# Digit searches with fixed thresholds for the capacity routing of an attention and mixture-of-experts kernel

## Chip, cores and metric

One NeuronCore of a Trainium2 chip. The metric is the device time of one execution in microseconds (us), the median of the runs shown.

## What is computed

Attention over 8 batches, 8 heads, 576 positions and head width 64, with a threshold on the scores, then a mixture of experts over the 4608 rows that come out. Each expert takes exactly 576 rows, in the order of the logits:

```python
scores = scale * q @ k^T
scores = where(scores >= max(scores) - tau, scores, -1e9)
x      = softmax(scores) @ v                     # 4608 rows of 512
logits = x @ w_gate                              # 4608 x 8
for (token, e) in descending order of logits:    # greedy assignment
    if token is free and expert e holds < 576 tokens: assign
for e in range(8):
    out[rows of e] = relu(x[rows of e] @ w1[e]) @ w2[e]
```

## The kernel before

**Stages.** The attention runs until about 446 us: 64 pairs of heads are worked in slots of two score tiles, with TensorE, VectorE and ScalarE in a pipeline written out by hand. GpSimd adds tau to each tile's maximum (`mx`, line 76, tile `nb`), which the masking on VectorE (`stt`, line 91) needs one slot later. Then eight FFN rounds follow, one per expert, each with 12 x 16 matmuls of layer 1 (line 884) and a layer 2 (line 916); every operand is split into a high and a low part, so the corrections (`H`, `w1l`, `w2l`, `xl`, made by `tensor_tensor` through line 429) run on VectorE beside the matmuls.

**Searches.** The greedy assignment is done in rounds: each token's key `b` is its best logit among the open experts; the largest threshold is searched at which some expert has 576 tokens with a key at or above it; that expert closes with those tokens, and the next round follows. The tokens lie as 128 partitions x 36 columns. A search (`phase`, line 648) has seven levels. One level: `step_cmp` compares all keys with 32 or 16 thresholds (VectorE, `cmp`); `step_cnt` counts per threshold and expert with nine matmuls (line 500) and copies the counts (`cn`, `cm` or `cs`, by how late the search is); `step_flag` sums them with small matmuls (lines 517 and 519) and sets a flag per threshold (`jka`); `step_n` counts the flags with another matmul (lines 535, 549) and derives the next thresholds. Levels 0 to 2 work with tables (`E`, 34 thresholds in fp32), levels 3 to 6 with `scalar_tensor_tensor` of 1152 fp32 elements, whose added offset stands in PSUM (search 0) or in a small tile `sd`. `pick` and `rank1` then give the expert `e`, `pack` gives the row list `idx` with one-hot compares (`poh`, line 610).

**Search 0** (`alone`) follows the attention directly. Its first 31 columns are prepared and compared in the attention's `tail` (line 321), the last five after the last logits. Beside it run 30 deferred row units (`xt_unit`, line 243): four transposes on TensorE, two evictions on ScalarE and a store of up to 260 KB to `xrows`, through two PSUM banks and eight buffers. A loop (lines 380 to 384) interleaves them by time in the program's own costs: a search step when its time has come, else a row unit each `XTY` us. The gather of expert 0's rows (line 798, GpSimd) needs `idx` and the stored rows; its first weights are loaded from the ScalarE queue (line 737).

**Searches 1 to 6** run beside the FFN matmuls. `place` (line 934) starts them one after the other; a search waits until the FFN three rounds before is done, and pauses while the rows of round 1 are taken. Each step yields a delay from costs written out in `Vec`, and the FFN matmuls issued until then stand in front of the step's matmuls in TensorE's queue. Corrections wait in `fills`: one is issued in each gap of a search, or when a matmul wants it.

```python
            twice=n=="tensor_tensor" and out.dtype==BF16 and ins[0].dtype==BF16      # L423
            t=max(s.free,s.now)
            if any(x.name==s.last for x in ins): t=max(t,s.done)
            s.free=t+0.07+big/(1.9 if twice else 0.96)/1000+(0.0 if acc is None else 0.09)
            s.done=s.free+0.115                                                      # L428
    def wait(s): return max(0.0,s.done-s.now)+s.lat                                  # L417
LATS=[0.15,0.35,0.35]+[0.6]*5                                                        # L701
```

Of the kernel before, what the change touches and what calls it, by code (L numbers as in the profile page):

```python
# [19 lines left out]
PPB=8; LTB=1; VTB=4; HOLD=1; XW=520; NBO=2; NDEF=4; XTB=4; XTY=1.05; XT0=-1.2; XRB=2  # L20


def attention(ctx, tc, qk, vl, wgd, xrows, xts, Lg, nb_batches, ident, dup, idle, R, after_first):
# [364 lines left out]
NC_=36; J=32; CAP=576; BIGS=8192.0; RC=1.5*2.0**28; NH=20; ADDS=3  # L388

def const_arrays():  # L390

    k=np.zeros((128,4096),np.float32); o={}; pos=0
    def put(name,a):
        nonlocal pos
        a=np.asarray(a,np.float32)
# [2 lines left out]
    e=[2.0**(-126+16*i) for i in range(16)]
    put("E1",np.array([-FMAX]+[-x for x in reversed(e)]+e+[FMAX]))
    put("pw",np.array([2.0**i for i in range(J+2)])); put("nw",np.array([2.0**-i for i in range(J+2)]))  # L400
    put("lev",2.0**(1-5.0*np.arange(1,6)))
    lw=np.tile(2.0**(1-5.0*np.arange(1,6)),(128,1)); lw[0,4]=0; put("lew",lw)
    put("io",np.arange(J+2)); put("io4",np.arange(J+2)/16)
# [29 lines left out]
class Router:  # L433
# [8 lines left out]
    def setup(s,ident):  # L442
# [9 lines left out]
        x=ident.rearrange("p (c t) -> p c t",c=4); V.tensor_reduce(s.own,x,axis=AX.X,op=ALU.add)  # L452
        with s.nc.allow_low_precision(reason="one term of each sum is not zero"): V.tensor_reduce(s.sum,x.rearrange("p c t -> p t c"),axis=AX.X,op=ALU.add)
    def consts(s):
        V=s.V; G=s.G
# [23 lines left out]
    def compare(s,E0,js,c0=0,c1=NC_):  # L479
        n=c1-c0  # L480
        s.V.tensor_tensor(s.cmp.rearrange("p (c j) -> p c j",j=J)[:,c0:c1,:js],s.b[:,c0:c1].unsqueeze(2).to_broadcast([128,n,js]),E0[:,1:js+1].unsqueeze(1).to_broadcast([128,n,js]),op=ALU.is_ge)
    def step_cmp(s,E):
        V=s.V; lv=E["lv"]; s.js=js=16 if lv in (0,1) else J
        if lv>1:


            o=1 if lv<5 else 0
            V.scalar_tensor_tensor(s.cmp.rearrange("p (c j) -> p c j",j=J),s.st[:,lv-2,o:o+J].unsqueeze(1).to_broadcast([128,NC_,J]),E["add"],s.b.unsqueeze(2).to_broadcast([128,NC_,J]),op0=ALU.add,op1=ALU.is_le)
            return
        s.compare(E["E"],js,31 if s.alone and lv<0 else 0)  # L490
        if lv==1:

            s.hb=s.wk.tile([128,5],BF16,name="hb"); V.tensor_scalar(s.hb,s.k("lew"),s.ab,None,op0=ALU.mult)
            s.st=s.wk.tile([128,4,J+2],F32,name="st"); s.lo=E["lo"]
            V.scalar_tensor_tensor(s.st,s.k("io").unsqueeze(1).to_broadcast([128,4,J+2]),s.ab,s.k("lev")[:,1:5].unsqueeze(2).to_broadcast([128,4,J+2]),op0=ALU.mult,op1=ALU.mult)
# [28 lines left out]
    def step_n(s,B):

        V=s.V
        lv=B["lv"]
        ps=s.ps()
        if lv>0:


            d=ps[:,0:1]
            for l in range(lv,0 if s.alone else lv-1,-1):
                k=32 if l==5 else 128
                s.T.matmul(d,s.hb[0:k,l-1:l].to_broadcast([k,128]),s.jk[:,8:9] if l==5 else s.fl[:,l+1:l+2],start=(l==lv),stop=(l==1 or not s.alone))
            if not s.alone and lv<5:
                sd=s.wk.tile([128,1],F32,name="sd",bufs=3)
                if lv==1: V.tensor_copy(sd,d)
                else: V.tensor_tensor(sd,B["add"],d,op=ALU.add)
                d=sd  # L540
            if lv<5: return {"add":d,"lv":lv+1}
            s.T.matmul(ps[:,1:10],s.ones[0:32],s.jk,start=True,stop=True)
            lo=s.wk.tile([128,1],F32,name="lo5",bufs=2)
            if s.alone: V.tensor_tensor(lo,s.lo,d,op=ALU.add)
            else: V.scalar_tensor_tensor(lo,d,B["add"],s.lo,op0=ALU.add,op1=ALU.add)
            return {"lo":lo,"lv":6,"full":ps}
        E2=s.wk.tile([128,J+2],F32,name="E",bufs=3)
        n=ps[:,0:1]
        s.T.matmul(n,s.ones,s.fl[:,lv+1:lv+2],start=True,stop=True)
        sm=s.wk.tile([128,2],F32,name="sm",bufs=3); lo=sm[:,0:1]  # L550
        jk=s.wk.tile([128,J+2],F32,name="jk2")
        V.scalar_tensor_tensor(jk,s.k("io"),n,B["E"],op0=ALU.is_equal,op1=ALU.mult,accum_out=lo)
        if lv==-1:

            V.tensor_scalar(E2,s.k("pw"),lo,FMAX,op0=ALU.mult,op1=ALU.min)
            V.scalar_tensor_tensor(E2,s.k("nw"),lo,E2,op0=ALU.mult,op1=ALU.max)
        else:
            s.ab=sm[:,1:2]
            V.scalar_tensor_tensor(s.ab,lo,-1.0,lo,op0=ALU.mult,op1=ALU.max)
            V.tensor_scalar(E2,s.k("io4"),s.ab,lo,op0=ALU.mult,op1=ALU.add)  # L560
        return {"E":E2,"lo":lo,"lv":lv+1}
# [499 lines left out]
```

## Time and profile before

| | us |
|---|---|
| median of three runs | 967.71 (966.82 to 968.75) |
| profiled execution, its own time | 965.63 |
| its span, first to last instruction | 963.9 |
| granted TensorE clock, mean | 0.996 |
| busy: TensorE, VectorE, ScalarE, GpSimd | 936.5, 775.7, 638.3, 277.7 |

A row of the profile gives engine, line, operation, tiles and shapes, and the time in us. In a timeline the first column is the start, the second the duration (a row with a count spans from the first start to the last end), and in brackets the idle time before and what ended it. PE is TensorE, DVE is VectorE, ACT is ScalarE, POOL is GpSimd, SP is the sync engine. VectorE operations of the searches and corrections all carry line 429, so they are told apart by their tiles.

### The profile page before, as it was taken

To read this page: it belongs to the slowest core of one execution; us is meant where nothing else is said; L and a number is where in the kernel's file an instruction comes from. 1 tells how busy PE (TensorE), PEld (TensorE's weight loads), DVE (VectorE), ACT (ScalarE), POOL (GpSimd) and SP (SyncE) were. 2 spreads that over 40 slices of the span, in tenths; PEclk is the share of its full clock that TensorE was granted. 3 is DMA by queue.
4 is the path that set the end of the run, shared out by engine and by line. 5 is a ranking of instruction groups with operands and counts; after the bars stand their busy time and mean duration, and the time that the engine had idled before them with its cause. 6 is when DMAs were issued, how large, how long until landed. Compare 5 with 4: busy or idle time off the path is not lost.

```text
span 963.9 us, 24282 instructions
## 1 busy us (share of the span) xinstructions
PE 936.5 (97%) x9182; PEld 700.8 (73%) x9182; DVE 775.7 (80%) x2177; ACT 638.3 (66%) x1301; POOL 277.7 (29%) x485
## 2 busy tenths in 40 slices
PE   7999999999999999998889999999999999999996
PEld 4565666566566656565778797897988979898994
DVE  8999999999999999996778787788897978536220
ACT  6999999999999999996645343443543525455430
POOL 3434354353534343340020302113041323310101
PEclk9999999999999999999999999999999999999999
DMA  6322252533432333205752505325342516530101
GB/s 260 124 101 88 85 195 93 205 127 111 168 111 101 125 102 123 88 2 193 251 181 74 191 18 173 107 90 175 105 154 94 168 49 215 183 103 32 39 12 44
DMA packets 36293, 117.02 MB, mean 121 GB/s; under 512 B 4304, under 2 KB 4944, under 8 KB 35664
## 3 DMA queue, kind: packets, MB, share of 16 engines
q1 hardware_dynamic: 28784, 93.89, 27.9%
q0 software_dynamic: 5888, 19.03, 6.3%
q10 hardware_dynamic: 1504, 2.54, 0.9%
q8 instruction: 73, 1.20, 0.5%
q14 instruction: 44, 0.36, 0.1%
HBM read 93.01 MB, written 21.38 MB: 119 GB/s over the span
## 4 chain that ended last, share of the span: by engine, by line
PE 84%; DVE 7%; issue 5%; DMA 2%; POOL 0%; ACT 0%; POOLq 0%; ACTq 0%; DVEq 0%
PE pf L884 19%; PE pf L916 18%; PE sc L70 15%; PE xo L156 14%; PE tb L99 9%; PE sc L99 2%; PE xo L166 2%; PE pt L825 1%; DVE cmp L429 1%; DVE z L75 1%; DVE pp L91 1%; PE rps L500 1%; DMA out_dram<-y,idx 1%; PE xo L178 1%; DMA xg<-xrows,idx 1%
## 5 line engine op out<-in xcount | busy, mean ns | idle before, releaser
L75 DVE TENSOR_SCALAR_CACHE_REDUCE z<-sc 128x576 f32<-128x576 f32 x288 | 205.9, 752 | 15.1 <-PE sc L70 13.1
L76 POOL TENSOR_SCALAR nb<-nb,wg 128x1 f32<-128x1 f32 x288 | 144.8, 504 | 248.1 <-DVE z L75 185.5
L87 ACT ACTIVATE pp<-z,nb 128x576 f32<-128x576 f32 x256 | 192.9, 773 | 24.0 <-DVE z L75 20.7
L91 DVE SCALAR_TENSOR_TENSOR pp<-z,nb,pp 128x576 f32<-128x576 f32 x256 | 200.0, 814 | 0.0
L916 PE MATMUL pf<-w2h,H 128*128 128x512 f32 x576 | 191.5, 398 | 1.9 <-DVE H L429 1.9
L70 PE MATMUL sc<-qk 64*128 64x288 f32 (+1 forms) x1280 | 177.8, 421 | 1.0 <-DVE z L75 0.8
L156 PE MATMUL xo<-pt,vt 128*64 128x320 f32 (+1 forms) x1024 | 155.7, 420 | 0.0
L117 ACT ACTIVATE pt<-tb 128x512 f32<-128x512 f32 x253 | 137.7, 591 | 1.9 <-PE tb L99 1.3
L916 PE MATMUL pf<-w2l,H 128*128 128x512 f32 x320 | 128.4, 401 | 0.4 <-DVE w2l L429 0.4
L924 POOL DMA_INDIRECT out_dram<-y,idx x40 | 44.2, 1105 | 289.4 <-ACT y L919 188.0
L916 PEld LDWEIGHTS pf<-w2h,H 128*128 128x128 f32 x576 | 107.4, 189 | 22.4 <-DVE H L429 2.3
L70 PEld LDWEIGHTS sc<-qk 64*128 64x128 f32 (+1 forms) x1280 | 93.1, 177 | 27.9 <-DVE z L75 3.9
L884 PE MATMUL pf<-xl,w1h 128*128 128x288 f32 (+2 forms) x512 | 110.1, 299 | 0.0
L884 PE MATMUL pf<-xh,w1h 128*128 128x288 f32 (+2 forms) x512 | 109.9, 299 | 0.1
L884 PE MATMUL pf<-xh,w1l 128*128 128x288 f32 (+2 forms) x512 | 110.0, 299 | 0.0
L99 PEld LDWEIGHTS tb<-ident,pp 64*128 64x128 f32 x2032 | 75.2, 140 | 44.9 <-issue 18.9
L156 PEld LDWEIGHTS xo<-pt,vt 128*64 128x64 f32 x1024 | 60.7, 136 | 58.4 <-issue 32.4
L919 ACT ACTIVATE y<-pf 128x512 f32<-128x512 f32 x40 | 23.9, 598 | 117.2 <-PE pf L916 111.7
L896 ACT ACTIVATE hf<-pf 128x576 f32<-128x576 f32 x56 | 36.5, 653 | 89.4 <-PE pf L884 83.5
L99 PE MATMUL tb<-ident,pp 64*128 64x64 f32 x2032 | 91.9, 227 | 3.3 <-ACT pt L117 3.0
L798 POOL DMA_INDIRECT xg<-xrows,idx x40 | 51.1, 1278 | 132.3 <-PE pf L884 45.7
L884 PEld LDWEIGHTS pf<-xh,w1h 128*128 128x128 f32 x512 | 81.8, 188 | 1.0 <-ACT xh L826 0.3
(206 smaller groups left out, 1358.2 us busy)
## 6 DMA issues: line engine op xcount, KB each, us to landing
qk<-qk_dram SPq DMA_DIRECT2D x31, 864.0 KB, 4.5
vt<-vl_dram SPq DMA_DIRECT2D x32, 576.0 KB, 3.7
w2s<-w_dram SPq DMA_DIRECT2D x32, 512.0 KB, 5.5
w1s<-w_dram SPq DMA_DIRECT2D x28, 512.0 KB, 5.8
xrows<-pp SPq DMA_DIRECT2D x24, 260.0 KB, 2.3
xts<-xt SPq DMA_DIRECT2D x2, 1152.0 KB, 5.6
pt<-xts SPq DMA_DIRECT2D x2, 1152.0 KB, 6.9
xrows<-xr SPq DMA_DIRECT2D x8, 260.0 KB, 2.2
```

The lines of the kernel that those rows point to most:

```text
L70: T.matmul(sc[o,f,:HS], kd["q",h][r,c], kd["k",h][r,:],start=True,stop=True)
L75: V.tensor_scalar(z,SC.pop(t)[:,:,:HS],-0.125,None,op0=ALU.mult,op1=ALU.min,accum_out=nb[:,0:1])
L76: G.tensor_scalar(nb[:,1:2],nb[:,0:1],taub[:,0:1],None,op0=ALU.add)
L87: A.activation(pview(t),ZB[t].rearrange("p a b -> p (a b)"),AF.Exp,bias=NBI[t][:,0:1],scale=-1.0)
L91: V.scalar_tensor_tensor(pv,ZB.pop(t).rearrange("p a b -> p (a b)"),NBI[t][:,1:2],pv,op0=ALU.is_le,op1=ALU.mult,accum_out=den_of(p)[:,p%4/ ...
L99: g=slice(64*r,64*r+64); T.transpose(o[:,r],x[r%len(x)][g],ident[g,g])
L117: else: A.activation(o,tb,AF.Copy)
L156: T.matmul(xo[64*h:64*h+64,:q.stop-q.start],v[:,f,128*u+64*h:128*u+64*h+64],PT[p][:,h,u,q],start=new,stop=last,skip_group_check=True)
L798: G.indirect_dma_start(out=x[:n],out_offset=None,in_=xrows,in_offset=IOA(ap=s["idx"][:n,t:t+1],axis=0))
L884: T.matmul(ps[:,h,:n],s[w][:,k,f*128:(f+1)*128],s[x][:,k,cols[h]],start=(i==0),stop=(i==11))
L916: T.matmul(ps[:,0,:],H[:,f,c:c+128],s[w][:,f],start=(f==0 and j==0),stop=e)
L924: G.indirect_dma_start(out=out,out_offset=IOA(ap=s["idx"][:n,t:t+1],axis=0),in_=y[:n],in_offset=None)
```

## The change

Each key's bits are turned into an unsigned order and cut into seven digits of 5, 5, 5, 5, 4, 4 and 4 bits (`digits`: three operations on 36 columns and three on 7 x 36). A level compares a bf16 number `e` per key with thresholds that never change (`th`): `e` starts as the first digit, and each level takes off the threshold that was found and adds the next digit, scaled by 1/64 per level. So a key above the found prefix stays above all thresholds, and one below it stays below. Level 0 of search 0 compares the fp32 keys with 32 fp32 thresholds (`E0`, by `compare`, with one instruction for whole groups of four columns and one for each cut group). Four levels have 32 thresholds, three have 16. In the first three searches `cmp` is laid out with four columns innermost, in the later ones as before with the thresholds innermost. The tables, `hb`, `st` and `sd` are gone. The thresholds and scales are built once, mostly on GpSimd (`consts`). The row units stand 0.9 instead of 1.05 us apart in the program's costs.

```diff
-PPB=8; LTB=1; VTB=4; HOLD=1; XW=520; NBO=2; NDEF=4; XTB=4; XTY=1.05; XT0=-1.2; XRB=2
+PPB=8; LTB=1; VTB=4; HOLD=1; XW=520; NBO=2; NDEF=4; XTB=4; XTY=0.9; XT0=-1.2; XRB=2
...
-        R.prep(0,31); R.compare(R.k("E1"),J,0,31)
+        R.prep(0,31); R.compare(0,31)
         both_ev(b,x[:,:,384:],slice(0,64),V); V.tensor_copy(rd[64:128,:,4],RD[b-1][64:128,:,4])
+        for g in R.digits(0,31): g()
...
+SHL=(0,5,10,15,20,24,28); SHR=(27,)*4+(28,)*3; JS=(32,)*4+(16,)*3; NL=7
...
     def consts(s):
...
+        s.th=[t("th%d"%l,[128,n,4],BF16) for l,n in enumerate(JS)]; s.unit=t("unit",[128,NL],BF16); s.sh=t("sh",[128,2,NL],I32)
+        G.iota(s.th[0],pattern=[[1,32],[0,4]],base=1,channel_multiplier=0,allow_small_or_imprecise_dtypes=True)
+        for l in range(NL):
+            G.memset(s.unit[:,l:l+1],64.0**-l)
+            for i,n in enumerate((SHL[l],SHR[l])): G.memset(s.sh[:,i,l:l+1],n)
+            if l: G.tensor_scalar(s.th[l],s.th[0][:,:JS[l]],64.0**-l,-64.0**-l if l==NL-1 else 0.0,op0=ALU.mult,op1=ALU.add)
...
+    def digits(s,c0=0,c1=NC_):
...
+        return [lambda: V.tensor_scalar(z,s.b[:,c0:c1],0.0,None,op0=ALU.add),
+            lambda: V.tensor_scalar(k,zi,31,-2**31,op0=ALU.arith_shift_right,op1=ALU.bitwise_or),
+            lambda: V.tensor_tensor(k,zi,k,op=ALU.bitwise_xor),
+            lambda: V.tensor_tensor(d,k.unsqueeze(1).to_broadcast([128,NL,n]),w(s.sh[:,0]),op=ALU.logical_shift_left),
+            lambda: V.tensor_tensor(d,d,w(s.sh[:,1]),op=ALU.logical_shift_right),
+            lambda: V.tensor_tensor(D,d,w(s.unit),op=ALU.mult)]
+    def compare(s,c0=0,c1=NC_):
...
+    def step_cmp(s,l):
+        V=s.V; s.js=m=JS[l]
+        if s.alone and l==0: s.compare(31); return
+        e=s.e if l else s.D[:,0]
+        if s.count>ADDS: V.tensor_tensor(s.cmp.rearrange("p (c j) -> p c j",j=J)[:,:,:m],e.unsqueeze(2).to_broadcast([128,NC_,m]),s.th[l][:,:,0].unsqueeze(1).to_broadcast([128,NC_,m]),op=ALU.is_ge)
+        else: V.tensor_tensor(s.cmp.rearrange("p (g j c) -> p g j c",j=J,c=4)[:,:,:m],e.rearrange("p (g c) -> p g c",c=4).unsqueeze(2).to_broadcast([128,9,m,4]),s.th[l].unsqueeze(1).to_broadcast([128,9,m,4]),op=ALU.is_ge)
...
+    def step_n(s,l):
+        V=s.V; ps=s.ps(); n=ps[:,0:1]; m=s.js; u=s.unit[0:m,l:l+1].to_broadcast([m,128])
+        if l<NL-1:
+            s.T.matmul(n,u,s.fl[0:m,l:l+1],start=True,stop=True)
+            e=s.wk.tile([128,NC_],BF16,name="e0",bufs=3)
+            V.scalar_tensor_tensor(e,s.e if l else s.D[:,0],n,s.D[:,l+1],op0=ALU.subtract,op1=ALU.add)
+            s.e=e; return
+        s.T.matmul(n,u,s.jk[0:m,8:9],start=True,stop=True)
+        s.T.matmul(ps[:,1:10],s.ones[0:m],s.jk[0:m],start=True,stop=True)
...
     def phase(s,last=False):
...
+            todo=s.digits(31 if s.alone else 0)
+            def work(n):
+                while n and todo: todo.pop(0)(); n-=1
+            if not s.alone: work(6)
...
+            for l in range(NL):
+                s.step_cmp(l); work(3); yield gap()
+                held(0.34); s.step_cnt(); work(2); yield gap()
                 if s.count<=ADDS: held(0.16)
+                s.step_flag(l); work(1); yield gap()
+                held(0.1); E=s.step_n(l)
                 if not s.alone: yield V.ease()
```

`pick` and `rank1` compare the last `e` instead of `b`. In `setup`, `own`, `sum` and `eye` are built in the new order of columns; `tri` takes the identity from SBUF instead of from the loaded constants, of which the tables are gone.

## Rows read from the trace of the kernel before

**Rows 1.** Busy time by stage, whole kernel. Columns: the stretch and its length, then busy us of PE, PEld (weight loads), DVE, ACT and POOL with their instructions, the granted clock, the share of the 16 DMA engines and GB/s.

```profile
8.00:60.00 52.00, 48.29 (x598) 28.76 (x598) 51.90 (x147) 47.24 (x89) 20.94 (x45) 1.00 0.42 152
60.00:440.00 380.00, 379.87 (x4828) 230.57 (x4825) 363.82 (x1014) 359.85 (x726) 156.70 (x344) 1.00 0.33 113
448.00:480.00 32.00, 26.86 (x347) 22.05 (x348) 22.07 (x77) 20.05 (x61) 0.00 (x0) 1.00 0.76 259
480.00:500.00 20.00, 16.19 (x175) 14.61 (x173) 14.16 (x42) 9.91 (x27) 6.58 (x6) 1.00 0.63 200
500.00:587.00 87.00, 86.61 (x669) 76.56 (x668) 73.43 (x201) 41.21 (x87) 11.23 (x11) 1.00 0.32 105
587.00:596.00 9.00, 7.14 (x47) 5.02 (x46) 5.15 (x18) 1.64 (x3) 4.24 (x4) 0.81 0.30 94
596.00:920.00 324.00, 323.83 (x2250) 285.90 (x2249) 231.00 (x637) 144.23 (x284) 71.78 (x62) 1.00 0.35 117
```

**Rows 2.** The chain of waits between 464 and 490 us, in order of time. Columns: start, length, engine, tile and line. L500 is the count, L247 a row unit's transposes, L519 and L535 the small matmuls, L250 and L251 a row unit's evictions.

```profile
464.64 1.44 DVE cmp L429
...
466.12 0.39 PE sc L500 x9
466.51 0.48 PE xo L247 x4
...
467.09 0.52 PE xo L247 x4
467.61 0.09 PE sc L535 x4
...
472.46 0.48 ACT pp L250
472.94 0.10 ACT pp L251
...
474.53 5.84 DMA w1s<-w_dram
...
480.62 2.29 POOL xg L798
...
488.82 1.23 PE pf L884 x6
```

**Rows 3.** Timeline of VectorE from 441 to 486 us: preparation of the keys, search 0, packing, and the first scaling of gathered rows.

```profile
441.74 0.42 DVE L429 TENSOR_TENSOR q<-Lg,b 128x248 bf16<-128x248 f32 x1
...
447.40 0.36 DVE L209 TENSOR_TENSOR lw<-sc,rd 128x64 f32<-128x64 f32 x2 [2.66 <-PE sc L99]
...
452.09 0.26 DVE L429 SCALAR_TENSOR_TENSOR jk<-cst,sc 128x34 f32<-128x34 f32 x1 [0.36 <-PE sc L549]
...
452.68 0.25 DVE L429 SCALAR_TENSOR_TENSOR E<-cst,sm,E 128x34 f32<-128x34 f32 x1
452.96 0.76 DVE L429 TENSOR_TENSOR cmp<-b,E 128x576 bf16<-128x576 f32 x1
...
471.13 0.15 DVE L429 TENSOR_TENSOR lo<-sm,sc 128x1 f32<-128x1 f32 x1 [0.75 <-PE sc L542]
...
471.93 0.15 DVE L429 TENSOR_SCALAR e<-m 128x1 int32<-128x1 f32 x1
...
474.17 0.76 DVE L429 TENSOR_TENSOR poh<-pio,prb 128x1152 bf16<-128x1152 bf16 x1
...
478.22 0.17 DVE L429 SCALAR_TENSOR_TENSOR idx<-cps,ih 128x5 int32<-128x5 f32 x1
...
485.29 0.69 DVE L429 TENSOR_TENSOR xg<-xg 128x512 f32<-128x512 f32 x1 [1.62 <-DMA xg<-xrows,idx]
```

**Rows 4.** What the sync engine's queue waited for between 430 and 500 us. Columns: total, times, longest. Line 773 stands behind the last row store.

```profile
SPq L773 <- DMA xrows<-pp: 5.4, 1, 5.4
```

**Rows 5.** Timeline of VectorE from 620 to 645 us: a compare of search 3 and the copy of its counts (`cs`), and two operations of the preparation of search 4.

```profile
621.02 1.42 DVE L429 SCALAR_TENSOR_TENSOR cmp<-st,sd,b 128x1152 bf16<-128x1152 f32 x1
623.55 0.15 DVE L429 COPY cs<-rps 32x8 f32<-32x8 f32 x1 [1.11 <-PE rps L500]
...
642.18 0.31 DVE L429 TENSOR_TENSOR q<-q,w8b 128x288 bf16<-128x288 bf16 x1
...
643.01 0.46 DVE L429 TENSOR_TENSOR oh<-q,qm 128x288 bf16<-128x288 bf16 x1
```

**Rows 6.** Timeline of all engines from 587 to 590 us: search 3's first compare and the layer 2 matmul that waits.

```profile
587.38 1.35 DVE L429 TENSOR_TENSOR cmp<-b,cst 128x1152 bf16<-128x1152 f32 x1
...
589.39 0.50 PE L916 MATMUL pf<-w2h,H 128*128 128x512 f32 x1 [1.86 <-DVE H L429]
```

**Rows 7.** Timeline of all engines from 34 to 40 us: GpSimd's constants, the delayed `nb`, and the masking on VectorE that needs it.

```profile
34.38 0.68 POOL L458 TENSOR_SCALAR w8b<-cst 128x8 bf16<-128x8 f32 x1
...
35.41 0.09 POOL L461 MEMSET fla<- 128x6 bf16 x1
35.47 0.39 POOL L463 IOTA pio<- 128x128 bf16 x1
...
35.94 0.30 POOL L464 TENSOR_SCALAR pio<-pio 128x128 bf16<-128x128 bf16 x1
...
37.01 1.17 POOL L76 TENSOR_SCALAR nb<-nb,wg 128x1 f32<-128x1 f32 x2
...
39.32 0.81 DVE L91 SCALAR_TENSOR_TENSOR pp<-z,nb,pp 128x576 f32<-128x576 f32 x1
```

More of the change, by code (lines that the diff above doesn't have):

```diff
@@ L397, in put @@
         k[:a.shape[0],pos:pos+a.shape[1]]=a; o[name]=(pos,a.shape[1]); pos+=a.shape[1]
[L398 to L403, printed above, removed]
+    top=[(n<<27)^(1<<31) if n>=16 else ~(n<<27)&0xffffffff for n in range(1,32)]
+    put("E0",np.append(np.array(top,np.uint32).view(np.float32),np.finfo(np.float32).max))
     put("w8",8-np.arange(8))
@@ L451, in setup @@
         s.own=t("own",[128,4],F32); s.sum=t("sum",[128,32],F32R)
-        x=ident.rearrange("p (c t) -> p c t",c=4); V.tensor_reduce(s.own,x,axis=AX.X,op=ALU.add)
-        with s.nc.allow_low_precision(reason="one term of each sum is not zero"): V.tensor_reduce(s.sum,x.rearrange("p c t -> p t c"),axis=AX.X,op=ALU.add)
+        V.tensor_reduce(s.own,x.rearrange("p j c -> p c j"),axis=AX.X,op=ALU.add)
+        with s.nc.allow_low_precision(reason="one term of each sum is not zero"): V.tensor_reduce(s.sum,x,axis=AX.X,op=ALU.add)
     def consts(s):
@@ L456, in consts @@
         t=lambda n,sh,dt:s.cp.tile(sh,dt,name=n)
-        s.tri=t("trib",[128,128],BF16); V.scalar_tensor_tensor(s.tri,s.k("eye"),BIGS,s.k("tri"),op0=ALU.mult,op1=ALU.add)
+        s.tri=t("trib",[128,128],BF16); V.scalar_tensor_tensor(s.tri,s.ident,BIGS,s.k("tri"),op0=ALU.mult,op1=ALU.add)
         s.w8=t("w8b",[128,8],BF16); G.tensor_scalar(s.w8,s.k("w8"),1.0,0.0,op0=ALU.mult,op1=ALU.add)
@@ L478, in prep @@
         V.tensor_tensor(s.oh[:,c0:c1],q,m.unsqueeze(2).to_broadcast([128,n,8]),op=ALU.is_equal)
[L479 to L495, printed above, removed]
+    def digits(s,c0=0,c1=NC_):
+        V=s.V; wk=s.wk; n=c1-c0
+        z=wk.tile([128,NC_],F32,name="z0",bufs=1)[:,:n]; k=wk.tile([128,NC_],I32,name="key",bufs=1)[:,:n]; d=wk.tile([128,NL,NC_],I32,name="dg",bufs=1)[:,:,:n]
+        if c0==0: s.D=wk.tile([128,NL,NC_],BF16,name="D",bufs=1)
+        D=s.D[:,:,c0:c1]; zi=z.bitcast(I32)
+        w=lambda a: a.unsqueeze(2).to_broadcast([128,NL,n])
+        return [lambda: V.tensor_scalar(z,s.b[:,c0:c1],0.0,None,op0=ALU.add),
[4 more added lines that the diff above has]
+            lambda: V.tensor_tensor(D,d,w(s.unit),op=ALU.mult)]
@@ new lines, in compare @@
+    def compare(s,c0=0,c1=NC_):
+        c=s.cmp.rearrange("p (g j c) -> p g j c",j=J,c=4)
+        t=s.k("E0")
+        while c0<c1:
+            g=c0//4; n=min(c1-c0,4-c0%4) if c0%4 or c1-c0<4 else (c1-c0)//4*4
+            k=max(n//4,1); w=min(n,4)
+            b=s.b[:,c0:c0+n].rearrange("p (g c) -> p g c",c=w)
+            s.V.tensor_tensor(c[:,g:g+k,:,c0%4:c0%4+w],b.unsqueeze(2).to_broadcast([128,k,J,w]),t.unsqueeze(1).unsqueeze(3).to_broadcast([128,k,J,w]),op=ALU.is_ge)
+            c0+=n
@@ L518, in step_flag @@
             else:
-                for c in range(4): s.T.matmul(n,s.eye[:,32*c:32*c+32],s.cn[:,8*c:8*c+8],start=(c==0),stop=(c==3))
-        if lv==1: V.tensor_scalar(s.st,s.st,s.lo,None,op0=ALU.add)
+                for c in range(4): s.T.matmul(n,s.eye[:,c],s.cn[:,8*c:8*c+8],start=(c==0),stop=(c==3))
         jk=s.wk.tile([32,9],BF16,name="jka"); s.jk=jk; m=s.js
-        fl=jk[:,8:9] if lv==5 else s.fl[0:m,lv+1:lv+2]
+        fl=jk[0:m,8:9] if l==NL-1 else s.fl[0:m,l:l+1]
         V.tensor_scalar(jk[0:m,0:8],n[0:m],CAP-0.5,None,op0=ALU.is_ge,op1=ALU.max,accum_out=fl)
[L524 to L561, printed above, removed]
@@ new lines, in step_n @@
+    def step_n(s,l):
[7 more added lines that the diff above has]
+        s.T.matmul(ps[:,1:10],s.ones[0:m],s.jk[0:m],start=True,stop=True)
+        lo=s.wk.tile([128,1],F32,name="lo",bufs=2); V.tensor_scalar(lo,n,-64.0**-l,None,op0=ALU.add)
+        return {"v":s.e,"lo":lo,"full":ps}
```

20 lines of the change are left out of this document (7 added, 13 removed).

## The prediction

> **What bounds the kernel now.** I read the busy time by stage first [rows 1]: TensorE is full from 60 to 440 us (379.87 of 380), from 500 to 587 (86.61 of 87) and from 596 to 920 (323.83 of 324). It is short in three places: 5.1 us between 448 and 480, 3.8 us between 480 and 500, and 1.9 us between 587 and 596, where the granted clock is also down to 0.81. Up to 60 us VectorE is the full engine (51.90 of 52). A change to the searches can gain only where TensorE is short; elsewhere it can at best cost nothing.
>
> Then the chain of waits between 464 and 489 us [rows 2]: one level of search 0 is a compare on VectorE (1.44), nine counting matmuls (0.39), one row unit (0.48), four small matmuls, another row unit (0.52) and the last matmuls (0.09). With hand-overs that is 3.07 us, and the row units hide the small VectorE operations between. Behind the search come the weights (5.84), the first gather of rows (480.62) and the first FFN matmul (488.82). The VectorE timeline [rows 3] has the search's ends: result lo at 471.13, expert e at 471.93, row list idx from 478.22 to 478.39. Behind its last row store the sync engine waits 5.4 us more until the stores have landed [rows 4], so they end well after the search.
>
> **Search 0, six levels.** The new compare has the operand kinds and the layout of poh, which takes 0.76 us for 1152 elements [rows 3]: I take 0.76 for 32 thresholds. For 16 thresholds (576 elements) I take 0.46, on the line between 0.31 for 288 [rows 5] and 0.76. A level gains a VectorE operation between the last matmul and the next compare; the nearest row, E of 128x34, takes 0.25. So a level goes from 3.07 to 3.07 - 0.68 + 0.25 = 2.64 us, or with 16 thresholds 2.34 us. From the first step operation (jk, 452.09) to lo there are now 19.0 us. Two of these six compare 576 elements in 0.76 already [rows 3], so what they gain is not the compare but jk and two E of 0.25 each. After: 3 x 2.64 + 3 x 2.34 = 14.9 us; minus 0.2 for the last level, whose five short matmuls become one; plus 2 x 0.25 where the program's own spacing puts two row units (0.98) in front of a 16-threshold count: 15.2 us.
>
> The first level gets longer: its compare of five columns becomes two instructions (+0.2), three digit operations stand in front of the count's copy (0.15 each by lo, some 0.3 uncovered), and one more row unit falls into it at the closer spacing (about +0.2): +0.7 us. The row units' own limit is ScalarE, 0.48 + 0.10 us of evictions a unit [rows 2]; at 30 units, 17.4 us, in some 20 us there is little left, and I add 0.3. Search 0 ends 19.0 - 15.2 - 0.7 - 0.3 = 2.8 us earlier. The row units don't fall behind: by the program's costs a level of 3.84 us holds 3.66 units at 1.05 now, and one of 3.47 or 3.16 us holds 3.85 or 3.5 at 0.9.
>
> The digits of the first 31 columns are six VectorE operations in the attention's tail, three of some 0.17 and three of 217 elements at up to 0.42 (q of 248 elements): 1.8 us, with 0.2 for the split compare. They lie in the 2.66 us that VectorE waits for the logits [rows 3]: nothing, but 0.6 us is all that is left of the cover.
>
> **From the search to the first FFN matmul.** The gather needs idx, the stored rows, and by the chain it follows the weights. idx and the weights' issue move with e: 2.8 us. The transfers have their own limit: 32 us at share 0.76 [rows 1] are 24.3 us of all 16 engines. Dense from 450 us on, two us into that stretch, they would end near 474, 6 us before the weights land now (480.37); if the closer rows only queue in front of the weights, the gate moves by 1 us. I take 2.8, because the weights land 8.4 us after e now, with the transfers already dense; ends 1.0 and 4.0. Search 1's six digit operations (3 x 0.17 + 3 x 0.42 = 1.8 us) and its faster compare (1.35 to 0.76 [rows 3, 6]) add 1.2 us to VectorE ahead of the first scaling of gathered rows, where it now waits 1.62 us for the gather [rows 3]. So nothing, unless the integer operations take twice that: then 0.9 us show.
>
> **The stall at 587 us.** The correction of the last block of H stands behind search 3's first compare (1.35) in VectorE's queue, and TensorE waits 1.86 us for it [rows 6]. Then the clock falls: 9 us at 0.81 lose 1.7 us more [rows 1]. Search 2 runs beside FFN 1, and its levels are spaced by the program's costs (0.07 + elements/960 us, elements/1900 where a compare counts as fast, and 0.115 more until it is done). Step and compare count 0.19 + 1.385 now, 0.22 + 0.79 or, with 16 thresholds, 0.22 + 0.49 after. So of the six levels that remain after the rows of FFN 1 are taken one shrinks by 0.56 and three by 0.86, and the two before them, which lose their table operations, by 0.52 and 0.77: 4.4 in all. Search 3's preparation comes that much earlier, before its six digit operations lengthen the block from 1.35 to 3.2 us. It would end near 586, before H is wanted. I take 1.2 of the 1.86 and the whole clock loss: -2.9. Ends: -3.6, and +1.9 if the block comes no earlier.
>
> **GpSimd's constants.** At 34.38 us GpSimd builds constants for 2.6 us, and the operand nb of a row of softmax tiles waits behind them until 37.01 [rows 7]. New there: one iota (0.39), six scalings (0.30 or less), 21 one-column memsets (0.09, or 0.06 by the next one's start): 0.4 + 1.6 + 1.3 = 3.3 us; ends 2.0 (were the memsets free) and 4.1. nb, ready near 37.6 now, would come near 40.9. VectorE needs it at 39.32 and has nothing else to do: a stall of 1.6 us where VectorE sets the pace. TensorE is nearly as full there, and from 60 us on it is the bound, so I count half: +0.8, ends 0 and +2.5. The changed one-time constants at the start end before the first scores and cost nothing.
>
> **Searches 3 to 6.** Their compare keeps the old layout: one key repeated for all thresholds innermost, and thresholds at a stride. A row shows what that costs: oh, bf16 with one operand repeated innermost, takes 0.46 for 288 elements, against 0.31 for q with plain rows [rows 5]. So the per-element time doubles and I take 1.35 for 1152 elements and 0.76 for 576. VectorE's work for such a search stays about the same: now one compare of 1.35, two of 0.76 and four of 1.42, 8.6 us; after, four of 1.35 and three of 0.76, 7.7, and 1.8 of digits. But the program's costs take it as fast: 0.68 and 0.37. Counting matmuls are placed by that, some 0.6 us nearer. Now the compare ends at 622.44, and the copy of the counts at 623.55 waits for a count of 0.39 [rows 2, 5], which so started near 623.12: 0.68 later. So about 0.1 is left at 16 levels and 0.3 at 12. VectorE is late by more than that in a few: +0.7, ends 0 and +8.
>
> The Trainium skill (Vector Engine (DVE) Microarchitecture Reference, section 5.1) says that a two-source 16-bit operation runs two elements a cycle only with step 1 innermost on all operands, and that an element read again and again as one source ran at one a cycle. The rows of oh and q agree; without this rule, at 0.76 for 1152 elements, the term would be 0 and the sum 0.7 us lower.
>
> **Sum.** -2.8 - 2.9 + 0.8 + 0.7 = -4.2 us. The profiled execution took 965.6 us (963.9 of span), 2.1 less than the median of 967.7. So 961.4 by that execution, 963.5 by the median.
>
> **Rivals.** (1) The stall at 587 stays, because search 2 is held by something else than its levels (it pauses while rows of FFN 1 are taken). For it: one unlucky order of two instructions decides. Then -1.3 us, 966.4. Chance 0.22. (2) The transfers are the limit: rows at the closer spacing fill the queues, the weights arrive 1 us earlier and not 2.8. For it: dense transfers now, the 5.4 us tail. Against it: share 0.76, not 1. Then -2.4: 965.3, on the bound of what can be told apart. Chance 0.10. (3) Slower: in searches 3 to 6 the counts are placed for a compare that runs at half the speed, and TensorE, which is full there, waits in its own queue. It decides from the point where the 0.68 us of slack is gone: with 0.5 us at 16 levels, 8 us, against 2.8 + 2.9 of gains. With 0.8 for the constants that is +3.1: 970.8. Against it: the slack is as large as the misjudged time. Chance 0.14. (4) The first three searches' compare isn't fast either; poh speaks against it. The six levels then take 3 x 3.23 + 3 x 2.64 = 17.6 us, the first level takes back 0.7, and search 0 gains 0.7 in all; search 2 gains too little to pass the stall: 967. Chance 0.02.
>
> The Trainium skill's rule above is what (3) rests on beside the rows; by it the compare is slow there for certain, and only the slack is open.
>
> **Numbers.** The forecast has 0.52, with a range of its own from 959.8 to 965.8: the gate at 4.0, the whole stall gone and no new cost give -7.6, about 960. A measurement here tells some 0.2% apart, 1.9 us. Faster: 0.52, 0.05 of (1) and 0.05 of (2), 0.62. Same: the rest of (1) and (2), and (4), 0.24. Slower: (3), 0.14. The range goes from 959.8 to 968.5 and leaves out (3) and little else.
>
> **What would show it.** In the changed profile: compares of 0.76 and 0.46 us in search 0 and 2.3 to 2.6 us per level; lo 2.8 us earlier than 471.1 (after the attention's own shift), the gather and the first FFN matmul with it; no wait of TensorE on H near 587 and clock 1.00 there; a VectorE wait on nb near 39 us; compares of 1.35 in searches 3 to 6 with counts right behind them. It is wrong if the gather stays, if the stall at 587 grows, or if TensorE waits for compares between 600 and 800 us by more than 2 us.

## The result: the change makes the kernel slower

| | before | after |
|---|---|---|
| median (six runs each), us | 968.5 (966.8 to 972.0) | 975.75 (973.4 to 977.4) |
| profiled execution, its span, us | 965.6, 963.9 | 973.4, 971.6 |
| mean granted clock | 0.996 | 0.995 |

The ratio is 1.007 (95% interval 1.0049 to 1.0092), against a forecast of 963.5 us. The stages show where, as [rows 1] do for before (columns as there):

```profile
8.00:60.00 52.00, 47.73 (x578) 27.89 (x578) 50.06 (x144) 45.78 (x87) 23.88 (x71) 1.00 0.43 153
448.00:480.00 32.00, 28.18 (x357) 22.70 (x350) 19.88 (x83) 22.73 (x65) 0.95 (x1) 1.00 0.74 260
480.00:500.00 20.00, 15.99 (x159) 14.57 (x157) 13.38 (x39) 6.86 (x19) 4.37 (x6) 0.91 0.67 218
500.00:587.00 87.00, 85.31 (x674) 75.41 (x674) 67.70 (x200) 40.24 (x87) 10.47 (x11) 1.00 0.31 102
587.00:596.00 9.00, 8.92 (x55) 6.67 (x54) 8.14 (x24) 4.51 (x9) 5.28 (x4) 1.00 0.25 66
596.00:920.00 324.00, 321.72 (x2186) 280.09 (x2185) 221.35 (x604) 138.98 (x273) 62.73 (x63) 1.00 0.35 117
```

The stall at 587 us is gone (8.92 of 9, clock 1.00). But TensorE's idle time explains little of 7.7 us of span, and a full TensorE can still be slow. So I compared milestones: the first FFN matmul, and the start of the last eviction of `y` in each round (line 919, after the change 911):

| us | before | after | difference |
|---|---|---|---|
| first FFN matmul | 488.82 | 489.75 | +0.9 |
| FFN 0 | 552.30 | 555.97 | +3.7 |
| FFN 1 | 616.26 | 621.23 | +5.0 |
| FFN 2 | 675.68 | 682.48 | +6.8 |
| FFN 3 | 734.28 | 743.28 | +9.0 |
| FFN 4 | 793.37 | 802.89 | +9.5 |
| FFN 5 | 849.99 | 857.88 | +7.9 |
| FFN 6 | 903.44 | 911.34 | +7.9 |
| FFN 7 | 954.46 | 962.36 | +7.9 |

The loss grows while searches run beside the FFN and stands still in rounds 6 and 7, which have none. (FFN 5 gives some back. The last two searches end 16 and 9 us earlier, so more of their work lies in earlier rounds, which would explain it.) Of FFN 0's 2.8 us, 1.7 are one wait of TensorE at 543 us (see the last section). What grows through the rounds is in TensorE's rows, and no duration shows it. First before, then after: a flag matmul (L535, now L543) between three layer 2 matmuls, with the weight load of the matmul behind it (PEld).

```profile
723.31 0.39 PE L916 MATMUL pf<-w2h,H 128*128 128x512 f32 x1
...
723.54 0.18 PE L535 MATMUL rps<-fla,hb 128*128 128x1 bf16 x1
723.54 0.20 PEld L916 LDWEIGHTS pf<-w2h,H 128*128 128x128 f32 x1
723.58 0.48 PE L916 MATMUL pf<-w2h,H 128*128 128x512 f32 x1
...
723.90 0.39 PE L916 MATMUL pf<-w2l,H 128*128 128x512 f32 x1
```

```profile
671.25 0.39 PE L908 MATMUL pf<-w2h,H 128*128 128x512 f32 x1
...
671.57 0.17 PE L543 MATMUL rps<-fla,unit 16*128 16x1 bf16 x1
671.67 0.19 PEld L908 LDWEIGHTS pf<-w2h,H 128*128 128x128 f32 x1
671.67 0.50 PE L908 MATMUL pf<-w2h,H 128*128 128x512 f32 x1
...
672.01 0.39 PE L908 MATMUL pf<-w2l,H 128*128 128x512 f32 x1
```

The small matmul lasts 0.18 and 0.17 us. Read start to start: from the first matmul to the last there are 0.59 us before and 0.76 after. Two layer 2 matmuls, 0.227 us from start to start elsewhere, are 0.45 of that, so the flag matmul costs TensorE 0.13 us before and 0.30 after. The form (rows contracted over, then columns of the weights) differs: 128*128 against 16*128. The new flags lie on 32 partitions, and `step_n` contracts over 32 or 16 rows where the old one contracted over 128. Over the 36 such matmuls beside the FFN rounds the medians are 3 + 39 + 85 ns (in front, itself, behind) before and 94 + 102 + 106 ns after: 175 ns more, 6.3 us in all. The weight load of the next matmul starts 2 ns behind the start of the flag matmul before (median of the 35 that the trace has) and 101 ns behind it after: it no longer overlaps the short matmul. That the form is the cause is tested next, in both directions.

### The profile page after: what moved, and what is told of

It is laid out like the page before. It is cut to its first block, busy times and chain, and to the rows that moved or that the text cites. A ratio compares the mean times of both kernels' runs of the same rounds, so it can differ in the third digit from the quotient of the medians.

```text
span 971.6 us, 24276 instructions
## 1 busy us (share of the span) xinstructions
PE 943.8 (97%) x9172; PEld 703.2 (72%) x9172; DVE 766.4 (79%) x2168; ACT 639.7 (66%) x1301; POOL 272.1 (28%) x513
## 4 chain that ended last, share of the span: by engine, by line
PE 80%; DVE 9%; issue 7%; DMA 2%; POOL 1%; ACT 1%; POOLq 0%; DVEq 0%
PE pf L908 18%; PE pf L876 17%; PE sc L70 14%; PE xo L156 13%; PE tb L99 8%; PE sc L99 2%; DVE z L75 2%; PE xo L166 1%; PE pt L817 1%; PE xo L247 1%; DVE pp L91 1%; PE rps L516 1%; DVE cmp L426 1%; PE xo L178 1%; DMA out_dram<-y,idx 1%
## 5 line engine op out<-in xcount | busy, mean ns | idle before, releaser
L916 POOL DMA_INDIRECT out_dram<-y,idx x40 | 40.0, 1000 | 327.7 <-ACT y L911 195.2
L876 PEld LDWEIGHTS pf<-xl,w1h 128*128 128x128 f32 x512 | 81.6, 188 | 0.4 <-DVE xl L426 0.2
```

What stands on the lines that cost most here:

```text
L876: T.matmul(ps[:,h,:n],s[w][:,k,f*128:(f+1)*128],s[x][:,k,cols[h]],start=(i==0),stop=(i==11))
L916: G.indirect_dma_start(out=out,out_offset=IOA(ap=s["idx"][:n,t:t+1],axis=0),in_=y[:n],in_offset=None)
```

## The experiments

Four sets of four kernels. Each set had its own runs of the kernel before (medians 968.6, 964.7, 967.9 and 965.1 us), so ratios are compared, and medians within a set alone.

**Flags over 128 rows** (`flags128`).

```diff
-s.fl=t("fla",[32,NL-1],BF16)
+s.fl=t("fla",[128,NL-1],BF16)
-s.T.matmul(n,u,s.fl[0:m,l:l+1],start=True,stop=True)
+s.T.matmul(n,s.unit[:,l:l+1].to_broadcast([128,128]),s.fl[:,l:l+1],start=True,stop=True)
```

> The changed kernel with one edit: the matmul that counts the flags of a level contracts over all 128 partitions (flags and scales of the rows above the thresholds are zero) and not over 32 or 16. Theory A (a matmul over 32 or 16 rows between matmuls over 128 rows costs TensorE 302 ns with what stands before and behind it, one over 128 rows 127 ns; 36 such matmuls beside the FFN rounds): 36 x 0.175 = 6.3 us less, about 969.5 us median, ratio to the kernel before near 1.001. Rival B (the loss is TensorE waiting for compares that the costs take as fast): no change, ratio 1.007. Rival C (GpSimd's constants and the clock after search 0 are most of it): no change, 1.007.

Measured: ratio 1.0025 (1.0014 to 1.0036). The medians of the 36 are 3 + 39 + 85 ns again. The same edit (`flags128_b`) with the change once more beside it (`after2`), in a later set:

> The changed kernel with flag matmuls over 128 rows once more, on the same chip as its base: 36 x 0.175 us = 6.3 us less than the base if nothing else moves; 4.6 us less (as the first run had it) if one of the waits that it meets next (rows of FFN 2, clock in the hand-over) takes back the rest.

Measured: 975.35 us for the change (1.0071), 970.43 for this (1.0022, 1.0009 to 1.0035). So 4.5 to 4.9 us by the medians: A holds, and about a quarter of its 6.3 us is taken back. B and C, which forecast no change, fall as the cause of this part. The 0.2% that the mended kernel is still slower than the kernel before has other causes.

**The mirror** (`before_flags32`): the kernel before, flags over 32 rows.

```diff
-k=32 if l==5 else 128
+k=32
-s.T.matmul(n,s.ones,s.fl[:,lv+1:lv+2],start=True,stop=True)
+s.T.matmul(n,s.ones[0:32],s.fl[0:32,lv+1:lv+2],start=True,stop=True)
```

> The mirror: the kernel before with one edit, its flag matmuls contract over 32 partitions in place of 128 (the last level's did so already). Nothing of the change is in it. Theory A: 36 such matmuls beside the FFN rounds at 175 ns more each, +6.3 us, ratio about 1.0065. Rivals B and C: within 0.2% of the kernel before.

Measured: ratio 1.0044 (1.003 to 1.0057), 4.2 us. The rows have 94 + 102 + 107 ns, with nothing of the change in the kernel:

```profile
673.23 0.62 PE L916 MATMUL pf<-w2h,H 128*128 128x512 f32 x2
673.78 0.17 PE L535 MATMUL rps<-fla,hb 32*128 32x1 bf16 x1
673.88 0.50 PE L916 MATMUL pf<-w2l,H 128*128 128x512 f32 x1
674.22 0.63 PE L916 MATMUL pf<-w2h,H 128*128 128x512 f32 x2
```

One thing of the other sign can be seen: TensorE still waits for H (1.8 us, until 591.95), but the clock doesn't fall behind it, which gives back the 1.7 us of [rows 1]. That this is what the median lacks of the 6.3 us is not shown, for the two profiled executions lie 7.0 us apart (965.6 and 972.6).

```profile
587.00:596.00 9.00, 7.15 (x59) 5.37 (x58) 6.96 (x21) 2.27 (x4) 2.03 (x3) 1.00 0.36 141
```

**Constants at the start** (`consts_early`): the block that builds `th`, `unit` and `sh` moved from `consts` to `setup`.

> The changed kernel with the new thresholds, scales and shifts built on GpSimd at the start (where it idles from 1.3 to 5.8 us) and not at 35 us. If the wait of VectorE for nb (1.9 us) carries through to the end: the attention's last logits come 1.4 us earlier (448.83 to 447.4) and the time is 974.3 us, ratio 1.0055. If TensorE makes it up: 975.7, 1.007.

Measured: ratio 1.0068 (1.0048 to 1.0087): it can't be told from the change. The trace shows a part of it: the wait for `nb` is gone and the last keys come at 449.8 us, against 450.76 after the change and 449.33 before.

**More filling matmuls** (`warm94`): `WARM=[30,6,94]`. Nobody uses the result of a filling matmul; it only keeps TensorE busy.

> The changed kernel with 94 in place of 64 filling matmuls behind the last one of search 0's packing, so that TensorE has work until search 1's first count, which the six digit operations delay (it idles 1.81 us there now). If that idle time brings the clock down (the granted clock from 485 to 490 us is 0.67): clock 1.00 there, nine counting matmuls 0.39 in place of 1.26 us, 26 filling ones 1.62 in place of 2.54, the first FFN matmul near 488.0 in place of 489.75 and the time 974.0, ratio 1.005. If the clock has another cause: no change, first FFN matmul at 489.8.

Measured: ratio 1.0109 (1.0091 to 1.0127), worse, the first FFN matmul at 493.14, and the clock fell all the same (0.56 from 485 to 490 us). The count started at 483.03, but its signal reached VectorE only at 486.66 (see the last section). Nothing on the clock follows, since TensorE idled even longer.

**Two ways to the wait at 602 us.** With the short matmuls mended, the largest wait of TensorE beside the FFN rounds is this (timeline of `flags128`):

```profile
600.46 0.69 DVE L426 TENSOR_TENSOR xg<-xg 128x512 f32<-128x512 f32 x1 [2.41 <-DMA xg<-xrows,idx]
601.18 0.26 DVE L426 SCALAR_TENSOR_TENSOR e<-e,rps,D 128x36 bf16<-128x36 bf16 x1
601.48 1.36 DVE L426 TENSOR_TENSOR cmp<-e,th 128x1152 bf16<-128x1152 bf16 x1
...
602.89 0.39 PE L516 MATMUL rps<-oh,cmp 128*128 128x32 bf16 x9 [3.49 <-DVE cmp L426]
```

VectorE waits in its queue for FFN 2's rows to land, the search step stands behind them, and TensorE's count behind that. `ga11`: `GA=[5.0,6.5,11.0,8.0]`.

> The changed kernel with flag matmuls over 128 rows (971.2 us), and one edit more: the scaling of FFN 2's gathered rows is placed 11 in place of 8 us (the program's costs) after the gather is issued. Theory D (with the old stall at 587 us gone, the scaling comes 4.9 us after the first gather issue in place of 7.3, VectorE waits in its queue for the rows to land, and the search step behind it makes TensorE wait 3.65 us at 602.9, after which the clock falls): both go, wait on that compare under 0.5 us, clock 1.00 from 600 to 615, 3.6 + 1.7 = 5 us less, about 966 us. Rival E (the compare itself, 1.36 us where 0.68 is planned, is late): at most 1 us less, 970.

Measured: ratio 0.9989 (0.9978 to 1.0), 3.5 us less than `flags128` where 5 were forecast. No wait for rows, 0.6 us on the compare, clock 1.00 from 600 to 610 us where `flags128` has 0.83. `priced` sets `twice` to false for the compare of searches 3 to 6:

> The changed kernel with flag matmuls over 128 rows (971.2 us), and one edit more: the program's costs take the compare of searches 3 to 6 at full length (1.27 in place of 0.68 us for 1152 elements). Rival E: the counts stand later, TensorE's waits for compares from 600 to 700 us (3.65, 0.31, 0.46, 0.57 us) go, with the clock loss 966 us. Theory D: only the small ones go (1.3 us, 970), since at 601 VectorE waits for rows.

Measured: ratio 1.0004 (0.9993 to 1.0014). VectorE still waits for the rows (2.1 us), as D says, but no count stands right behind it, and from 600 to 700 us TensorE waits for nothing. The time lies between the two forecasts. Both are part of it: the rows make the wait, and the price decides whether a count meets it.

**Digits behind the scalings** (`defer`).

```diff
-if s.alone and l==0: s.compare(31); return
+if s.count<3 and l==0: s.compare(31 if s.alone else 0); return
...
-scale(4); s["lows"](1,(2,3))
+scale(4); s["lows"](1,(2,3)); R.work(6)
```

> The changed kernel with flag matmuls over 128 rows (971.2 us), and one edit more: search 1's first level compares the fp32 keys with the fp32 table, as search 0 does, and its six digit operations stand behind the scalings of expert 0's rows. If those operations ahead of the first count cost the gain of search 0 (TensorE idle 1.8 us, then 3 to 7 us at half clock): the count starts near 482.4 in place of 484, the clock is 1.00 from 480 to 500, the first FFN matmul near 488 in place of 490.5, 2 us less: 969. If the gather itself is late: the first scaling waits for it, under 0.5 us less, 971.

Measured: ratio 1.0041 (1.0027 to 1.0054), no better than `flags128` (1.0025), where 2 us less were forecast. In the trace the hand-over is what was forecast, with clock 1.00 from 480 to 500 us:

```profile
482.07 0.39 PE L516 MATMUL rps<-oh,cmp 128*128 128x32 bf16 x9 [0.38 <-DVE cmp L426]
482.89 1.62 PE L636 MATMUL cps<-trib,onesb 128*128 128x128 bf16 x26
487.33 0.74 PE L877 MATMUL pf<-xh,w1h 128*128 128x256 f32 x4
```

But the six operations now stand ahead of the next level's compare, for which TensorE waits 2.2 us at 494.85 (1.0 in `flags128`), and the wait by the rows, at 598 us, is 3.3 us. What the hand-over gains doesn't reach the end.

**All together** (`all4`): flags over 128 rows, constants at the start, `ga11`, `priced` and `defer`.

> All edits together: flag matmuls over 128 rows, scaling of FFN 2's rows at 11, compares priced in full, search 1's digits behind the scalings, constants on GpSimd at the start. If the four causes are separate: 971.2 - 5 (rows of FFN 2) - 1 (small waits) - 2 (hand-over) - 1.4 (constants) = 962 us, ratio 0.993 to the kernel before. If they hide one another: 965 to 968.

Measured: ratio 0.9956 (0.9942 to 0.997), faster than both kernels; first FFN matmul at 485.47. Of the 9 us expected beyond `flags128` it has 6.7 (1.0025 to 0.9956). No run separates what `defer`, which alone gained nothing, has in it.

**The spacing.** `best` adds the last level's pair over 128 rows and splits the digits (three ahead of `scale(1)`); `best_105` is that with `XTY=1.05`.

> All edits of the fourth run of the last set, and three more: the last level's two matmuls contract over 128 rows too (7 x 0.165 us = 1 us), three of search 1's digit operations stand in the 0.7 us in which VectorE waits for the second row tile, and the program counts the other three before the next step (TensorE waits 2.4 us at 493 us for that compare; 1 us is left as in the kernel before). Theory: 2.4 us less than that run's ratio of 0.9956, 0.993. If TensorE's later waits take it back: 0.9956.

> The same with the deferred row units 1.05 in place of 0.9 apart in the program's costs, as before the change. If the closer spacing carries the gain of search 0 (at 1.05 and the shorter levels more row units are left behind the search, and the gather waits for their stores): rows stored later, first FFN matmul 1 to 2 us later, ratio 0.2% above the run beside it. If the searches' levels carry it: the same within 0.1%.

Measured: 0.9965 (0.9951 to 0.9979) and 0.9938 (0.9923 to 0.9954). `best` is no better than `all4`: TensorE has new waits of 1.7 us at 539 and 1.5 and 1.3 us at 802 to 804 us. The spacing looked like a second cause, so it was tried alone, four ways.

> The kernel before with one edit: row units 0.9 in place of 1.05 apart (the change's second part alone). Theory F (between two row units a level's small matmuls wait for the transposes of 0.5 us; closer units stretch search 0, which took 19.7 us from the last keys to lo at 0.9 and 17.9 at 1.05 in the last two runs, and the gather gains nothing by it): lo 1 to 2 us later than 471.13, time up 1 to 2 us, ratio 1.001 to 1.002. Rival G (rows stored earlier let the gather start earlier): first FFN matmul 1 us earlier, ratio 0.999.

> The changed kernel with one edit: row units 1.05 apart as before (the change's first part alone). Theory F: lo 1.8 us earlier than 470.74, and if it carries through to the first FFN matmul 2 to 3 us less than the change, ratio 1.004 to 1.005. Rival G: rows left over behind the search, the gather 1 to 2 us later, ratio 1.008.

> The changed kernel with row units 1.05 apart and flag matmuls over 128 rows. If the short matmuls cost what the earlier pairs showed (4.6 and 4.9 us), that much less than the run without them beside it: ratio 1.000 by theory F, 1.003 by rival G.

> The kernel with four mending edits that had the ratio 0.9956 (flags over 128 rows, scaling of FFN 2's rows at 11, compares priced in full, digits behind the scalings, constants early), with row units 1.05 apart. Theory F: 2 to 3 us less, ratio 0.993. If the 3 us between the last two kernels were single waits of other places (539 and 802 us): within 0.1% of 0.9956.

Measured: `before_090` 0.9999 (0.999 to 1.0008), `after_105` 1.0072 (1.0057 to 1.0087), `flags128_105` 1.0027 (1.0016 to 1.0038), `all4_105` 0.994 (0.9928 to 0.9952). In the time the spacing does nothing that can be told apart, neither to the kernel before nor to the change (1.0072 against 1.007), so the change's loss comes from the searches. The flags are worth 4.5 us a third time (1.0072 to 1.0027).

The traces show more: the first half of theory F holds. From the last keys (the last reduction to `b`) to lo search 0 takes, in us:

| | units 1.05 apart | 0.9 apart |
|---|---|---|
| kernel before | 21.8 | 22.9 (`before_090`) |
| the change | 18.3 (`after_105`) | 20.0 |
| with flags over 128 rows | 18.0 (`flags128_105`) | 19.8 |
| `all4` | 18.0 (`all4_105`) | 19.8 |

So closer units cost search 0 of the change 1.7 us. What F has wrong is that the time carries through. In `after_105` the first FFN matmul is 1.1 us earlier than in the change (488.62), but near 600 us TensorE waits 2.8 us for a compare and the clock is 0.69 from 600 to 605 us. `all4_105` has no such wait: 1.4 us of gain at the first FFN matmul (484.05 against 485.47) are 1.3 at the end (span 956.8 against 958.0), though the intervals of the two ratios overlap. G falls: the last row unit ends later (473.84 against 471.32), but the gather is issued no later (478.77 against 479.05), and in `before_090` it is no earlier (480.89, before 480.62). What lies between the profiles of `best` and `best_105` is mostly single waits: the one at 539 us, and 2.8 against 1.8 us near 802. `all4_105` is the fastest kernel here beside `best_105`.

## Why the prediction was wrong

**Search 0: the levels priced rightly, the closer row units too low.** Compares and the added operation are as forecast; a level of 32 thresholds takes 2.74 us (forecast 2.64), the three of 16 take 2.75, 2.41 and 2.85 (forecast 2.34, and 0.5 more in all for row units), and lo comes at 470.74:

```profile
454.75 0.76 DVE L426 TENSOR_TENSOR cmp<-e,th 128x1152 bf16<-128x1152 bf16 x1
457.20 0.26 DVE L426 SCALAR_TENSOR_TENSOR e<-e,sc,D 128x36 bf16<-128x36 bf16 x1 [0.46 <-PE sc L543]
...
465.77 0.46 DVE L426 TENSOR_TENSOR cmp<-e,th 128x576 bf16<-128x576 bf16 x1
467.89 0.26 DVE L426 SCALAR_TENSOR_TENSOR e<-e,sc,D 128x36 bf16<-128x36 bf16 x1 [0.43 <-PE sc L543]
...
470.74 0.16 DVE L426 TENSOR_SCALAR lo<-sc 128x1 f32<-128x1 f32 x1 [0.48 <-PE sc L548]
```

From the last keys to lo it takes 20.0 us (450.76 to 470.74), before 21.8: 1.8 gained, 2.8 forecast. `after_105` shows where the rest went. With the old spacing it takes 18.3 us (451.48 to 469.80), so the shorter levels alone gain 3.5, and the closer row units take back 1.7, for which the prediction had 1.0 (0.2, 0.3 and twice 0.25).

```profile
469.80 0.16 DVE L426 TENSOR_SCALAR lo<-sc 128x1 f32<-128x1 f32 x1 [0.45 <-PE sc L548]
```

**The hand-over: failed at "so nothing, unless the integer operations take twice that".** They took what was forecast (0.17 to 0.20 and 0.42 us) and the first gather is issued earlier (479.05 against 480.62), although the last keys come 1.43 us later. But the first scaling of its rows starts at 485.47, without a wait ([rows 3]: 485.29, behind a wait of 1.62): all the cover is used up. What I didn't follow is the other queue. Search 1's count on TensorE stands behind the digits, and the scaling on VectorE stands behind the copy of that count. The change first, then the kernel before:

```profile
480.07 0.18 DVE L426 TENSOR_SCALAR z<-b 128x36 f32<-128x36 f32 x1
...
481.64 0.42 DVE L426 TENSOR_TENSOR D<-dg,unit 128x252 bf16<-128x252 int32 x1
482.09 0.76 DVE L426 TENSOR_TENSOR cmp<-D,th 128x1152 bf16<-128x1152 bf16 x1
482.90 0.39 PE L516 MATMUL rps<-oh,cmp 128*128 128x32 bf16 x9 [1.81 <-DVE cmp L426]
484.19 0.19 DVE L426 CAST cn<-rps 128x32 fp32r<-128x32 f32 x1 [1.34 <-PE rps L516]
484.58 2.68 PE L636 MATMUL cps<-trib,onesb 128*128 128x128 bf16 x26
...
489.75 0.51 PE L876 MATMUL pf<-xh,w1h 128*128 128x256 f32 x2
```

```profile
481.88 0.39 PE L500 MATMUL rps<-oh,cmp 128*128 128x32 bf16 x9 [0.37 <-DVE cmp L429]
...
482.70 1.62 PE L647 MATMUL cps<-trib,onesb 128*128 128x128 bf16 x26
```

TensorE idles 1.81 us, then 1.14 more (0.9 of it between the end of the count and the start of its copy, which the kernel before hasn't: see the last section), and then its granted clock is 0.67 from 485 to 490 us, the lower of its two levels for part of it: 26 filling matmuls take 2.68 us, before and in `defer` 1.62. From the last keys to the first FFN matmul there are 39.0 us (before 39.5, `defer` 35.8): 0.5 gained, where 2.8 was forecast and `defer` shows that it was there. In the change's trace the chain of waits from lo to this matmul runs through VectorE, TensorE and one ScalarE copy, no longer through the weights or the gather.

**The stall at 587 us: right, but what is late next was not named.** The wait and the clock loss are gone (8.92 of 9). In the kernel before, FFN 2's rows had more time to land: their scaling came 7.3 us after the first gather issue (592.07 to 599.40), now 5.0 (589.81 to 594.78). I put that down to the stall, which no run tests alone. VectorE now waits for the rows, 1.6 us in two waits, and the step behind lets TensorE wait at 601.5. First before, then after:

```profile
599.40 1.28 DVE L429 TENSOR_TENSOR xg<-xg 128x512 f32<-128x512 f32 x2
```

```profile
599.07 0.69 DVE L426 TENSOR_TENSOR xg<-xg 128x512 f32<-128x512 f32 x1 [0.83 <-DMA xg<-xrows,idx]
599.79 0.26 DVE L426 SCALAR_TENSOR_TENSOR e<-e,rps,D 128x36 bf16<-128x36 bf16 x1
600.09 1.36 DVE L426 TENSOR_TENSOR cmp<-e,th 128x1152 bf16<-128x1152 bf16 x1
...
601.50 0.39 PE L516 MATMUL rps<-oh,cmp 128*128 128x32 bf16 x9 [1.49 <-DVE cmp L426]
```

**GpSimd's constants: mechanism right, size off.** The burst is 4.0 us longer (3.3 forecast), VectorE waits 1.94 us, and most of it stays: the last keys come 1.43 us later, where I counted half a stall (+0.8). Other traces agree. In the ten traces with these constants built at 35 us the last keys come from 450.76 to 451.75, in the eight others from 449.31 to 450.45. The time alone can't tell this term from nothing.

```profile
41.06 2.03 POOL L76 TENSOR_SCALAR nb<-nb,wg 128x1 f32<-128x1 f32 x4
41.38 0.82 DVE L91 SCALAR_TENSOR_TENSOR pp<-z,nb,pp 128x576 f32<-128x576 f32 x1 [1.94 <-POOL nb L76]
```

**Searches 3 to 6: the compare was right (1.36 us for 1152 elements), the slack about right** (from 600 to 700 us TensorE waits 2.0 us for compares, 1.5 of it behind the rows; 0.5 is left, for +0.7). But rival (3), which came out nearest to the measured time, is right for a small part only: `flags128` leaves the compares as they are and takes away 4.5 to 4.9 us. Only with the flags mended are the waits for compares larger (4.2 us from 600 to 700 us), and then pricing them is worth 2.0 us (`priced`).

**The step that failed.** The part "Searches 3 to 6" counted VectorE's work and the slack of the counts, and had no term for TensorE's own small matmuls, though the diff shows `s.fl[0:m]` and `unit[0:m]` as its operands. For searches 1 and 2, in which 12 of the 36 stand, no part had one. "What bounds the kernel now" read TensorE as full from 500 to 587 and from 596 to 920 us and said that a change there "can at best cost nothing"; what a dearer mix of instructions costs there was put at nothing without a reason. It is 6.3 us by the rows and 4.5 to 4.9 in the kernel's time. The kernel before had a sign of it: its last level's pair contracts over 32 rows, with the same 94 ns in front and 105 behind.

Beside it, the hand-over's "So nothing" failed. Added up from the rows of the two profiles, the forecast of 961.4 us missed the measured 973.4 by these terms: flags 6.3, everything up to the first FFN matmul 2.9 (-2.0 forecast, +0.9 measured), the wait at 543 us 1.7, the wait at 601.5 us 1.5, less 0.7 for the stall (3.6 gained, 2.9 forecast) and 0.2 for the other compares. That is 11.5 of 12.0 us. It is a sum over one execution of each kernel, and of its terms only the flags were measured alone on the change.

Rivals (1), (2) and (4) didn't come: the stall went, the gather no longer waits for the weights, and the compare is fast. None of the three signs came that the prediction named for being wrong (TensorE waits 2.0 us for compares from 600 to 800 us, on the bound it gave), since none of them looked at what TensorE's own instructions cost. With the edits of `all4` the ratio is 0.9956, 4 to 5 us below the kernel before, near the -4.2 forecast for the change. That is luck: `all4` has no burst of constants, which the forecast counted, and other waits.

The Trainium skill has a rule for it (TensorEngine Tiling (Array Packing), Key Properties): going from one tiling mode of the array to another drains TensorE. The traces fit it for matmuls over fewer rows and give the size, 302 against 127 ns per matmul; for fewer columns they show no such cost (see the last section). Another page of the Trainium skill (TensorE: Matmul & The Clock Gate, Why this matters for your kernels) has it that one matmul over 32 rows takes as long as one over 128; here that holds for its own duration (0.17 and 0.18 us) and not for what stands around it.

What stays open: why 6.3 us by the rows are 4.2 to 4.9 in the time. In the mirror's profile the clock doesn't fall near 592 us; in `flags128` the wait near 602 us is 3.5 us where the change has 1.5, with a clock of 0.83 from 600 to 610. No run shows that this is the whole difference.

## What to carry to other kernels

Read TensorE's cost of an instruction from start to start of its neighbours; its own duration hid a factor of 2.4. Where an edit makes a small operand smaller, check whether the number of partitions contracted over changes between matmuls that use all 128, and pad with zeros if it does. For each operation added to an engine follow the first consumer on every queue, not the one that was critical before, and when a stall goes, list what had been using its time.

## What the runs showed of the hardware

A matmul over 16 or 32 rows among matmuls over 128 takes 302 ns of TensorE's time, one over 128 rows 127 ns, in both kernels and with the edit in either direction. Transposes of 64 rows (64*128) show it too, 96 ns in front and 108 behind. A restriction to 32 columns costs nothing of the kind: the sums over `c8n` (128*32) cost 0 + 29 + 85 ns.

Among row gathers a count's signal sometimes comes late. In the trace of the change the count ends at 539.08, its consumer starts at 541.39, and TensorE then waits for the rows that VectorE scales behind that ("remote" and "issue": the view has no releaser):

```profile
538.69 0.39 PE L516 MATMUL rps<-oh,cmp 128*128 128x32 bf16 x9
541.39 0.19 DVE L426 TENSOR_TENSOR cm<-rps,own 128x32 f32<-128x32 f32 x1 [2.66 <-remote]
...
543.14 0.43 PE L817 MATMUL pt<-ident,xg 64*128 64x64 f32 x4 [1.69 <-issue]
```

The same wait of VectorE, 2.0 to 2.7 us, stands in `after2`, `flags128`, `flags128_b`, `consts_early`, `warm94` and `best`; a longer one of 3.7 us in `warm94` at 486.66 and one of 3.2 in the mirror at 602.1; none in `ga11` or the kernel before. A shorter one is in the hand-over of the change: the count ends at 483.3, its copy starts at 484.19. The cause was not found.
